# Decode attention and MLP on one core: the MLP's first product moved behind the last contraction, and the output product moved into a section of its own

## The chip, the cores and the metric

The kernel runs on one core of a Trainium2 chip. The core has TensorE (PE in the profile, its weight loads PEld), VectorE (DVE), ScalarE (ACT), GpSimd (POOL), SyncE (SP) and 16 DMA engines, which carry data between HBM and the on-chip memory SBUF. TensorE writes to PSUM. The metric is the device time of one execution in microseconds (us); lower is better. All numbers are float32.

## The reference

One decode step for B = 4 rows of D = 512, with H = 32 heads of 128, and a cache of S = 4096 positions per row and head. Cut to what matters:

```python
xn = layernorm(x)                                  # (4, 1, 512)
# attention on the caches
q = (xn @ wq) as (4, 32, 1, 128)
p = softmax(q . k_cache * 128 ** -0.5)             # over 4096 positions
a = (p . v_cache) as (4, 1, 4096) @ wo             # (4, 1, 512)
# second branch: token mixing, then an MLP of width 1792
x1 = xn + shifted(gelu(layernorm(xn) @ w1)) @ w2   # one position: every shift moves it out, so x1 = xn
m = x1 + gelu(layernorm(x1) @ w3) @ w4
return x + a + m
```

With one position the shifts leave only padding, so w1 and w2 are not needed. The two caches hold 4 x 32 x 4096 x 128 floats each, 268 MB, and each element is used once.

## The kernel before

The 128 pairs of row and head are worked in 32 groups of 4 (`NG`, `HG`). A group's K and its V are 8.4 MB each, laid over 128 partitions. Three buffers of 8.4 MB (`slots` S0, S1, S2) hold everything large: K alternates between S1 and S0, V goes to S2. All large loads are issued by SP, in one queue, in the order in which SP's program has them.

Per group, DVE multiplies K by the query (line 347), sums over the head's 128 elements (line 349) and finds the maximum. ACT makes the softmax weights `pw` and their sums `rs` (line 258). PE contracts `pw` with V in 32 matmuls (`contract`, line 177) into the PSUM tile `pv`. ACT copies `pv` to `os`, and PE's `outputs` (line 183) makes the sums (`ones` x `rs`) and picks the diagonal blocks of `os` with `sel`; ACT copies these to `OS`. PE, ACT and DVE run this in hardware loops (`nc.Fori`).

Behind the loops comes the tail. The last V goes to S1. w3 and w4 go to S2 when its last V is used. wo goes to S0 when the last K is used, in the pieces of `PIECES` (line 72), each with a semaphore of its own. For every row b, DVE normalises `OS` and spreads it into `lt` (lines 359 to 363), PE's `spread` (line 192) turns it by a matmul, and ACT copies it to `X`, the left operand of the product with wo.

The order of the tail is written out by hand, engine by engine, with semaphores between them:

- PE: `spread` of rows 0 to 2, the last group's contraction, its `outputs`, `spread` of row 3, the MLP's first product (x1T x w3 into `pb`, line 211), the second product (gT x w4 into `y`, line 218), the product `ident` x `base` that puts x + xn into `total`, then the product with wo. wo has 32 chunks. Chunks 0 to 23 (`CUT`) are added to `y` in four rows of tiles, chunks 24 to 31 to `total` with four matmuls each. Behind chunk 27, `y`, which ACT has copied to `os` (line 288), is added to `total` by four matmuls with `sel`.
- ACT: the weights, the copies of X for rows 0 to 2, the last group's copies to `os` and `OS`, X for row 3, the copy of `pb` to `hs` (line 283), tanh (line 286), the copy of `y`, two output stores.
- DVE: the normalising of rows 0 to 3, three steps of gelu (lines 366 to 368), three more behind tanh (lines 370 to 372, the last writes gT), and the copy of `total` to `res` (line 374).
- SP: two output stores behind `res`.

All of this is one section (line 119), a block in which every engine has its own program. At its end the engines meet: each drains and signals, POOL releases them, and SP collects a second round of signals. A second section holds one wait of SP, for the output stores (line 377). Then the kernel ends with a further meeting and the clearing of semaphores.

Of the kernel before, what the change touches and what calls it, by code (L numbers as in the profile page):

```python
# [20 lines left out]
def decode_block(ctx: ExitStack, tc: tile.TileContext, x, k, v, wq, wo, w3, w4, out):  # L21
# [47 lines left out]
    def take(e, s, n=1):  # L69
        e.wait_ge(s, n).then_inc(s, -n)  # L70

    PIECES = ((0, 16), (16, 24), (24, 28), (28, 31), (31, 32))
    CUT = 24
    s_x, s_w3, s_w4, s_v, s_vl, s_out = (sem(n) for n in ("sx", "sw3", "sw4", "sv", "svl", "sout"))
    s_wq = [sem(f"swq{n}") for n in range(2)]
# [35 lines left out]
    def part(t):  # L111
        return slice(t * P, (t + 1) * P)

    def store(e, tt):
        e.wait_ge(d_r, 1)
        for t in tt:
            e.dma_start(out_r[:, part(t)], res[32 * t:32 * t + B, :]).then_inc(s_out, 16)

    with tc.tile_critical(no_gpsimd_drain=True), nc.Block(no_gpsimd_drain=True) as block:

        @block.sync
        def _(e):
            def load_k(g):
                e.dma_start(KS[g % 2][:, :], group(kf, g)).then_inc(s_k[g % 2], 16)

            wq_r = wq.rearrange("(p c) n -> p c n", p=P)
            for n in range(2):
                c = slice(n * NC // 2, (n + 1) * NC // 2)
                e.dma_start(wq_sb[:, c, :], wq_r[:, c, :]).then_inc(s_wq[n], 16)
            load_k(0)  # L130
            e.wait_ge(d_Q, 1)
            load_k(1)
            for g in range(NG - 1):
                if g > 0:
                    take(e, v_free)
                e.dma_start(S2[:, :], group(vf, g)).then_inc(s_v, 16)
                if g + 2 < NG:
                    take(e, k_free[g % 2])
                    load_k(g + 2)
            take(e, k_free[0])  # L140
            e.dma_start(S1[:, :], group(vf, NG - 1)).then_inc(s_vl, 16)
            take(e, v_free)
            e.dma_start(w3_sb, w3.rearrange("(p c) f -> p c f", p=P)).then_inc(s_w3, 16)
            e.dma_start(w4_sb, w4.rearrange("(p m) n -> p m n", p=P)).then_inc(s_w4, 16)
            take(e, k_free[1])
            wo_r = wo.rearrange("(p c) n -> p c n", p=P)
            for n, (c0, c1) in enumerate(PIECES):
                e.dma_start(wo_sb[:, c0:c1, :], wo_r[:, c0:c1, :]).then_inc(s_wo[n], 16)
            store(e, (0, 1))

        @block.gpsimd
        def _(e):
# [7 lines left out]

        @block.tensor
        def _(e):
            def mm(o, l, r, start, stop):
                return e.matmul(o, l, r, start=start, stop=stop)  # L164

            e.wait_ge(d_xT, 1)
            for c in range(NC):
                if c % (NC // 2) == 0:
                    e.wait_ge(s_wq[c // (NC // 2)], 16)
                w = wq_sb[:, c, :].rearrange("p (n j h d) -> p n h j d", n=2, j=JB // 2, h=HG)  # L170
                for n in range(2):
                    for h in range(HG):
                        i = mm((pa, pb)[n][32 * h:32 * h + 32, :], xnT[:, c, :], w[:, n, h], c == 0, c == NC - 1)
                    if c == NC - 1:
                        i.then_inc(p_q, 1)

            def contract(V):
                for g in range(G4):
                    t = g % 4
                    i = mm(pv[32 * t:32 * t + 32, :], pw[:, g, :], V[:, 4 * g:4 * g + 4, :], g < 4, g >= G4 - 4)  # L180
                return i

            def outputs(done):
                i = mm(oz[:, HG:2 * HG], ones[:, :], rs[:, :], True, True)
                if done is not None:
                    i.then_inc(done, 1)
                take(e, a_os)
                for m in range(4):
                    i = mm(oz[:, 0:HG], os[:, m, :], sel[:, HG * m:HG * m + HG], m == 0, m == 3)
                i.then_inc(p_oz, 1)  # L190

            def spread(b):
                take(e, d_lt)
                mm(pa[:, 32 * b:32 * b + 32], lt[:, :, :], sel[:, :], True, True).then_inc(p_x, 1)

            with nc.Fori(0, NG - 1, 1, engines=[ET.PE]):
                take(e, s_v, 16)
                take(e, a_w)
                contract(V3).then_inc(p_pv, 1)
                outputs(v_free)  # L200
            for b in range(B - 1):
                spread(b)
            take(e, a_w)
            e.wait_ge(s_vl, 16)
            contract(VL).then_inc(p_pv, 1)
            outputs(None)
            spread(B - 1)
            e.wait_ge(s_w3, 16)
            for c in range(NC):
                for t in range(4):  # L210
                    i = mm(pb[32 * t:32 * t + 32, :FT], x1T[:, c, :], w3_sb[:, c, t * FT:(t + 1) * FT],
                           c == 0, c == NC - 1)
            i.then_inc(p_up, 1)
            e.wait_ge(s_w4, 16)
            e.wait_ge(d_g, 1)
            for m in range(NF):
                t = m % 4
                mm(y[32 * t:32 * t + 32, :], gT[:, 32 * m:32 * m + 32], w4_sb[:, m, :], m < 4, False)
            mm(total[:, 0:P], ident[:, :], base[:, :], True, False)
            e.wait_ge(a_X, 1)  # L220
            for n, (c0, c1) in enumerate(PIECES):
                e.wait_ge(s_wo[n], 16)
                for c in range(c0, c1):
                    if c < CUT:
                        t = (c + 2) % 4
                        i = mm(y[32 * t:32 * t + B, :], X[:, c, :], wo_sb[:, c, :], False, c >= CUT - 4)
                        if c == CUT - 1:
                            i.then_inc(p_y, 1)
                    else:
                        for t in range(4):  # L230
                            i = mm(total[32 * t:32 * t + B, 0:P], X[:, c, :], wo_sb[:, c, part(t)], False, c == WC - 1)
                if c1 == 28:
                    e.wait_ge(a_y, 1)
                    for t in range(4):
                        mm(total[32 * t:32 * t + 32, 0:P], sel[:, :], os[:, t, :], False, False)
            i.then_inc(p_tot, 1)

        @block.scalar
        def _(e):
# [22 lines left out]
            def outputs(o):  # L262
                take(e, p_pv)
                e.copy(os[:, :, :], pv[:, :].rearrange("p (m d) -> p m d", m=4)).then_inc(a_os, 1)  # L264
                take(e, p_oz)
                return e.copy(o, oz[:, 0:2 * HG].unsqueeze(1))  # L266

            def spread(b):
                take(e, p_x)
                return e.copy(X[:, :, b], pa[:, 32 * b:32 * b + 32])  # L270
# [6 lines left out]
            e.drain().then_inc(a_end, 1)  # L277
            for b in range(B - 1):
                spread(b).then_inc(a_lt, 1)
            outputs(OS[:, NG - 1:NG, :]).then_inc(a_end, 1)  # L280
            spread(B - 1).then_inc(a_X, 1)
            e.wait_ge(p_up, 1)
            e.copy(hs.rearrange("p (m i) -> p m i", i=32),
                   pb[:, :FT].rearrange("p (i m) -> p m i", i=32)).then_inc(a_up, 1)
            e.wait_ge(d_u, 1)
            e.activation(gt, gu, AF.Tanh, scale=GELU_A).then_inc(a_t, 1)
            e.wait_ge(p_y, 1)
            e.copy(os[:, :, :], y[:, :].rearrange("p (m d) -> p m d", m=4)).then_inc(a_y, 1)
            store(e, (2, 3))

        @block.vector
        def _(e):
# [60 lines left out]
                    own(e.transpose(mt[:, :], mx[:, :]))  # L353
                    e.tensor_reduce(st[:, 1:2], mt[:, :], axis=AX.X, op=ALU.max, negate=True).then_inc(d_m, 1)  # L354

            for b in range(B):
                e.wait_ge(a_end, 2 if b == B - 1 else 1)
                o = OS[:, b * JB:(b + 1) * JB, :]
                own(e.reciprocal(rec[:, :, :], o[:, :, HG:]))  # L359
                own(e.tensor_mul(ot[:, :, :], o[:, :, 0:HG], rec[:, :, :]))  # L360
                if b > 0:
                    e.wait_ge(a_lt, b)
                e.tensor_mul(lt[:, :, :], ot[:, :, :].rearrange("p j h -> p (j h)").unsqueeze(2).to_broadcast([P, H, 4]),
                             mask[:, :].unsqueeze(1).to_broadcast([P, H, 4])).then_inc(d_lt, 1)
            e.wait_ge(a_up, 1)
            own(e.tensor_mul(gu, hs, hs))
            own(e.tensor_scalar(gu, gu, GELU_B, 1.0, op0=ALU.mult, op1=ALU.add))
            e.tensor_mul(gu, gu, hs).then_inc(d_u, 1)
            e.wait_ge(a_t, 1)
            own(e.tensor_scalar(gt, gt, 1.0, 0.5, op0=ALU.add, op1=ALU.mult))  # L370
            own(e.tensor_mul(hs, hs, gt))
            e.transpose(gT, hs).then_inc(d_g, 1)  # L372
            e.wait_ge(p_tot, 1)
            e.tensor_copy(res[:, :], total[:, 0:P]).then_inc(d_r, 1)  # L374

    with tc.tile_critical(no_gpsimd_drain=True):
        nc.sync.wait_ge(s_out, 64)


# [26 lines left out]
```

## Time and profile before

| | |
|---|---|
| median of 3 runs | 1310.01 us (1309.46 to 1312.22) |
| the profiled execution's own time | 1309.42 us |
| its span, first to last instruction | 1307.6 us |
| DVE busy | 1166.0 us (89%) |
| PE busy | 364.1 us (28%) |
| ACT busy | 98.7 us (8%) |
| read from HBM | 561.02 MB, 429 GB/s over the span |

The page's idle column names what ended an engine's wait; `q` behind an engine's name is its sequencer, which handles waits, branches and DMA issues. In a timeline a row is start (us from the span's start), duration (us), engine, line, operation, tiles, shape and count; a row with a count stands for several instructions merged, and its duration reaches from the first start to the last end. A DMA issue's duration is that of the issue; when the data lands stands in the DMA view. A float32 matmul shows as two instructions. All PE rows have the line of the small helper that issues matmuls, so they are told apart by their tiles. The granted clock of PE is given as a share of full speed.

### The profile page before, as it was taken

The page shows a single profiled execution, that of the slowest core. Times are in us where ns is not written, and L with a number is a line of the kernel's source. Part 1 is how long each engine was busy: PE and PEld are TensorE (multiplying, and loading weights), DVE is VectorE, ACT ScalarE, POOL GpSimd, SP SyncE. Part 2 cuts the span into 40 slices and gives each one's busy share as a digit, 9 for nine tenths or more (in the row PEclk, how much of TensorE's full clock was granted, in tenths as well). Part 3 has the DMA queues.
Part 4 walks back from the last instruction along what each step waited for, and adds up shares of the span by engine and source line. Part 5 has one row for each costly group of instructions (what it writes and reads, how often), then busy time and mean ns, then how long its engine had stood idle before and what let it go on. Part 6 is the DMA issues. An engine that isn't in the chain of part 4 may idle for free. (4 is left out here: it accounts for less than half of the span.)

```text
span 1307.6 us, 6922 instructions
## 1 busy us (share of the span) xinstructions
PE 364.1 (28%) x2622; PEld 130.6 (10%) x2622; DVE 1166.0 (89%) x308; ACT 98.7 (8%) x334; POOL 2.1 (0%) x9
## 2 busy tenths in 40 slices
PE   2032123332113333212333212333311333321256
PEld 0010011110001111001111000111100111100022
DVE  3799999999999999999999999999999999999961
ACT  0000000000000000000000000000000000000010
POOL 0000000000000000000000000000000000000000
PEclk9565566665566666566666556666655666655669
DMA  9999999999999999999999999999999999999997
GB/s 418 417 440 425 443 423 445 421 445 421 445 421 447 421 445 425 441 425 441 429 437 429 437 429 437 429 439 433 433 433 433 437 429 441 425 443 423 443 417 298
DMA packets 10582, 561.11 MB, mean 429 GB/s; under 512 B 1200, under 2 KB 1216, under 8 KB 1488
## 3 DMA queue, kind: packets, MB, share of 16 engines
q1 hardware_dynamic: 10528, 561.00, 99.3%
q8 instruction: 3, 0.05, 0.0%
q10 hardware_dynamic: 48, 0.04, 0.0%
q14 instruction: 3, 0.02, 0.0%
HBM read 561.02 MB, written 0.01 MB: 429 GB/s over the span
## 5 line engine op out<-in xcount | busy, mean ns | idle before, releaser
L347 DVE TENSOR_TENSOR slot<-slot,qb 128x16384 f32<-128x16384 f32 x32 | 551.2, 17226 | 42.4 <-DVEq L70 42.4
L349 DVE TENSOR_REDUCE sc<-slot 128x128 f32<-128x16384 f32 x32 | 551.0, 17220 | 10.5 <-DVEq L70 10.5
L164 PE MATMUL ps<-slot,pw 128*32 128x512 f32 x2048 | 293.5, 737 | 881.1 <-PEq L70 881.1
L164 PEld LDWEIGHTS ps<-slot,pw 128*32 128x32 f32 x2048 | 80.5, 132 | 1068.6 <-issue 1068.5
L258 ACT ACTIVATE pw<-sc,st 32x128 f32<-32x128 f32 x128 | 67.3, 526 | 307.1 <-ACTq L70 305.6
L264 ACT COPY os<-ps 128x512 f32<-128x512 f32 x32 | 18.8, 586 | 798.4 <-ACTq L70 798.4
L164 PE MATMUL ps<-sel,os 128*128 128x4 f32 x256 | 32.8, 252 | 18.1 <-PEq L70 18.1
L164 PEld LDWEIGHTS ps<-sel,os 128*128 128x128 f32 x256 | 31.0, 191 | 19.9 <-issue 19.9
L258 ACT ACTIVATION_READ_ACCUMULATOR pw<-sc,st 32x1 f32 x128 | 26.2, 205 | 0.0
L164 PE MATMUL ps<-slot 128*32 128x512 f32 x92 | 14.8, 788 | 27.8 <-DVE slot L326 22.5
L359 DVE RECIPROCAL rec<-OS 128x32 f32<-128x32 f32 x4 | 1.4, 349 | 14.4 <-ACT OS L266 12.1
L345 DVE STREAM_TRANSPOSE qb<-qx 128x128 f32<-128x128 f32 x32 | 10.0, 312 | 4.7 <-DVEq L70 0.2
L351 DVE TENSOR_REDUCE st<-sc 128x1 f32<-128x128 f32 x32 | 9.2, 286 | 4.7
L164 PE MATMUL ps<-rs,ones 128*128 128x4 f32 x64 | 12.3, 263 | 0.0
L164 PEld LDWEIGHTS ps<-rs,ones 128*128 128x128 f32 x64 | 9.5, 188 | 26.8 <-issue 26.8
L374 DVE COPY res<-ps 128x128 f32<-128x128 f32 x1 | 0.3, 291 | 13.1 <-PE ps L164 13.1
L342 DVE COPY qx<-Q 128x128 f32 x32 | 7.3, 227 | 4.8 <-issue 4.6
L306 DVE TENSOR_REDUCE st<-slot 128x1 f32<-128x512 f32 x2 | 1.4, 686 | 11.3 <-DMA slot<-in_A_x_dram 11.3
L353 DVE STREAM_TRANSPOSE mt<-mx 128x32 f32<-128x32 f32 x32 | 6.8, 211 | 4.7
L354 DVE TENSOR_REDUCE st<-mt 128x1 f32<-128x32 f32 x32 | 5.9, 186 | 4.8 <-DVEq L70 2.1
L352 DVE COPY mx<-st 128x32 f32<-128x32 f32 x32 | 5.8, 182 | 4.7
L266 ACT COPY OS<-ps 128x8 f32 (+1 forms) x32 | 5.3, 166 | 43.7 <-ACTq L70 43.7
(53 smaller groups left out, 49.7 us busy)
## 6 DMA issues: line engine op xcount, KB each, us to landing
slot<-in_A_wq_dram SPq DMA_DIRECT2D x2, 4096.0 KB, 17.2
slot<-in_B_w_dram SPq DMA_DIRECT2D x2, 3584.0 KB, 22.2
slot<-in_A_wo_dram SPq DMA_DIRECT2D x1, 4096.0 KB, 30.5
slot<-in_A_wo_dram SPq DMA_DIRECT2D x1, 2048.0 KB, 35.0
slot<-in_A_wo_dram SPq DMA_DIRECT2D x1, 1024.0 KB, 37.0
slot<-in_A_wo_dram SPq DMA_DIRECT2D x1, 768.0 KB, 38.4
slot<-in_A_k_cache_dram SPq DMA_DIRECT2D x32, 42.3
slot<-in_A_v_cache_dram SPq DMA_DIRECT2D x32, 28.9
```

The source lines that it names most:

```text
L164: return e.matmul(o, l, r, start=start, stop=stop)
L258: i = e.activation(o, sc[r, :].rearrange("p (g w) -> p g w", w=4), AF.Exp, bias=st[r, 1:2], scale=1.0, accum_out=rs[r, h:h + 1])
L264: e.copy(os[:, :, :], pv[:, :].rearrange("p (m d) -> p m d", m=4)).then_inc(a_os, 1)
L266: return e.copy(o, oz[:, 0:2 * HG].unsqueeze(1))
L342: own(e.tensor_copy(qx[:, :].rearrange("p (h r) -> p h r", h=4), Q[:, bass.ds(g + n, 1), :].rearrange("p o h -> p (o h)").unsqueeze(2) .to ...
L345: own(e.transpose(qb[:, :], qx[:, :]))
L347: own(e.tensor_tensor(out=K, in0=K, in1=qb[:, :].unsqueeze(1).to_broadcast([P, C, DH]), op=ALU.mult))
L349: e.reduce_sum(sc[:, :], K, axis=AX.X).then_inc(d_self, 1)
L351: own(e.reduce_max(st[:, 0:1], sc[:, :], axis=AX.X), 2)
L352: own(e.tensor_copy(mx[:, :], st[:, 0:1].to_broadcast([P, 32])))
L353: own(e.transpose(mt[:, :], mx[:, :]))
L354: e.tensor_reduce(st[:, 1:2], mt[:, :], axis=AX.X, op=ALU.max, negate=True).then_inc(d_m, 1)
```

## The change

Four things are done.

- The MLP's first product stands on PE directly behind the last group's contraction; `outputs` and `spread` of row 3 come after it. ACT copies `os`, then `hs`, then `OS`, then does tanh, then X for row 3. DVE does the first three gelu steps ahead of row 3's normalising, and the other three behind it.
- `ident` x `base` comes ahead of the second product.
- wo's first piece of 16 chunks is loaded as two of 8, with a semaphore each. SP issues six pieces in place of five.
- The section with the loops ends behind the second product. The product with wo, the copy of `y`, the copy to `res` and the four stores stand in the second section, which has no block and no loops. PE, ACT and DVE thus pass the meeting at the block's end, and the waits at the second section's entry, ahead of wo. The wait `a_X` in front of wo is gone, since ACT signals the block's end behind the copy of X.

The order of the instructions within wo's product is as before. The diff, cut to its core (`mm` moved out of the tensor program and given the engine as its first argument):

```diff
-    PIECES = ((0, 16), (16, 24), (24, 28), (28, 31), (31, 32))
+    PIECES = ((0, 8), (8, 16), (16, 24), (24, 28), (28, 31), (31, 32))
...
             contract(VL).then_inc(p_pv, 1)
-            outputs(None)
-            spread(B - 1)
             e.wait_ge(s_w3, 16)
             (first product)
             i.then_inc(p_up, 1)
+            outputs(None)
+            spread(B - 1)
+            mm(e, total[:, 0:P], ident[:, :], base[:, :], True, False)
             e.wait_ge(s_w4, 16)
             e.wait_ge(d_g, 1)
             (second product)
-            mm(total[:, 0:P], ident[:, :], base[:, :], True, False)
-            e.wait_ge(a_X, 1)
-            (product with wo)
...
# scalar
-            outputs(OS[:, NG - 1:NG, :]).then_inc(a_end, 1)
-            spread(B - 1).then_inc(a_X, 1)
+            take(e, p_pv)
+            e.copy(os[:, :, :], pv[:, :].rearrange("p (m d) -> p m d", m=4)).then_inc(a_os, 1)
             e.wait_ge(p_up, 1)
             e.copy(hs..., pb...).then_inc(a_up, 1)
+            take(e, p_oz)
+            e.copy(OS[:, NG - 1:NG, :], oz[:, 0:2 * HG].unsqueeze(1)).then_inc(a_end, 1)
             e.wait_ge(d_u, 1)
             e.activation(gt, gu, AF.Tanh, scale=GELU_A).then_inc(a_t, 1)
-            e.wait_ge(p_y, 1)
-            e.copy(os[:, :, :], y[:, :]...).then_inc(a_y, 1)
-            store(e, (2, 3))
+            spread(B - 1).then_inc(a_X, 1)
...
# vector
-            for b in range(B):
+            for b in range(B - 1):
+                normalised(b)
             (three gelu steps)
+            normalised(B - 1)
             e.wait_ge(a_t, 1)
             (three gelu steps)
-            e.wait_ge(p_tot, 1)
-            e.tensor_copy(res[:, :], total[:, 0:P]).then_inc(d_r, 1)
...
     with tc.tile_critical(no_gpsimd_drain=True):
+        e = nc.tensor
+        for n, (c0, c1) in enumerate(PIECES):
+            e.wait_ge(s_wo[n], 16)
+            (the same loop over wo's chunks as before)
+        i.then_inc(p_tot, 1)
+        nc.scalar.wait_ge(p_y, 1)
+        nc.scalar.copy(os[:, :, :], y[:, :]...).then_inc(a_y, 1)
+        nc.vector.wait_ge(p_tot, 1)
+        nc.vector.tensor_copy(res[:, :], total[:, 0:P]).then_inc(d_r, 1)
+        for e, tt in ((nc.sync, (0, 1)), (nc.scalar, (2, 3))):
+            e.wait_ge(d_r, 1)
+            for t in tt:
+                e.dma_start(out_r[:, part(t)], res[32 * t:32 * t + B, :]).then_inc(s_out, 16)
         nc.sync.wait_ge(s_out, 64)
```

More of the change, by code (lines that the diff above doesn't have):

```diff
@@ L112, in part, with mm @@
         return slice(t * P, (t + 1) * P)
[L114 to L117, printed above, removed]
+    def mm(e, o, l, r, start, stop):
+        return e.matmul(o, l, r, start=start, stop=stop)
     with tc.tile_critical(no_gpsimd_drain=True), nc.Block(no_gpsimd_drain=True) as block:
@@ L148, in _ @@
                 e.dma_start(wo_sb[:, c0:c1, :], wo_r[:, c0:c1, :]).then_inc(s_wo[n], 16)
-            store(e, (0, 1))
         @block.gpsimd
@@ L162, in _ @@
         def _(e):
-            def mm(o, l, r, start, stop):
-                return e.matmul(o, l, r, start=start, stop=stop)
             e.wait_ge(d_xT, 1)
@@ L172, in _ @@
                     for h in range(HG):
-                        i = mm((pa, pb)[n][32 * h:32 * h + 32, :], xnT[:, c, :], w[:, n, h], c == 0, c == NC - 1)
+                        i = mm(e, (pa, pb)[n][32 * h:32 * h + 32, :], xnT[:, c, :], w[:, n, h], c == 0, c == NC - 1)
                     if c == NC - 1:
@@ L179, in contract @@
                     t = g % 4
-                    i = mm(pv[32 * t:32 * t + 32, :], pw[:, g, :], V[:, 4 * g:4 * g + 4, :], g < 4, g >= G4 - 4)
+                    i = mm(e, pv[32 * t:32 * t + 32, :], pw[:, g, :], V[:, 4 * g:4 * g + 4, :], g < 4, g >= G4 - 4)
                 return i
             def outputs(done):
-                i = mm(oz[:, HG:2 * HG], ones[:, :], rs[:, :], True, True)
+                i = mm(e, oz[:, HG:2 * HG], ones[:, :], rs[:, :], True, True)
                 if done is not None:
@@ L188, in outputs @@
                 for m in range(4):
-                    i = mm(oz[:, 0:HG], os[:, m, :], sel[:, HG * m:HG * m + HG], m == 0, m == 3)
+                    i = mm(e, oz[:, 0:HG], os[:, m, :], sel[:, HG * m:HG * m + HG], m == 0, m == 3)
                 i.then_inc(p_oz, 1)
@@ L193, in spread @@
                 take(e, d_lt)
-                mm(pa[:, 32 * b:32 * b + 32], lt[:, :, :], sel[:, :], True, True).then_inc(p_x, 1)
+                mm(e, pa[:, 32 * b:32 * b + 32], lt[:, :, :], sel[:, :], True, True).then_inc(p_x, 1)
             with nc.Fori(0, NG - 1, 1, engines=[ET.PE]):
@@ L210, in _ @@
                 for t in range(4):
-                    i = mm(pb[32 * t:32 * t + 32, :FT], x1T[:, c, :], w3_sb[:, c, t * FT:(t + 1) * FT],
+                    i = mm(e, pb[32 * t:32 * t + 32, :FT], x1T[:, c, :], w3_sb[:, c, t * FT:(t + 1) * FT],
                            c == 0, c == NC - 1)
             i.then_inc(p_up, 1)
+            outputs(None)
+            spread(B - 1)
+            mm(e, total[:, 0:P], ident[:, :], base[:, :], True, False)
             e.wait_ge(s_w4, 16)
@@ L217, in _ @@
                 t = m % 4
-                mm(y[32 * t:32 * t + 32, :], gT[:, 32 * m:32 * m + 32], w4_sb[:, m, :], m < 4, False)
-            mm(total[:, 0:P], ident[:, :], base[:, :], True, False)
-            e.wait_ge(a_X, 1)
[L221 to L236, printed above, removed]
+                mm(e, y[32 * t:32 * t + 32, :], gT[:, 32 * m:32 * m + 32], w4_sb[:, m, :], m < 4, False)
         @block.scalar
@@ L284, in _ @@
                    pb[:, :FT].rearrange("p (i m) -> p m i", i=32)).then_inc(a_up, 1)
+            take(e, p_oz)
+            e.copy(OS[:, NG - 1:NG, :], oz[:, 0:2 * HG].unsqueeze(1)).then_inc(a_end, 1)
             e.wait_ge(d_u, 1)
             e.activation(gt, gu, AF.Tanh, scale=GELU_A).then_inc(a_t, 1)
-            e.wait_ge(p_y, 1)
-            e.copy(os[:, :, :], y[:, :].rearrange("p (m d) -> p m d", m=4)).then_inc(a_y, 1)
-            store(e, (2, 3))
+            spread(B - 1).then_inc(a_X, 1)
         @block.vector
@@ L354, in _, with normalised @@
                     e.tensor_reduce(st[:, 1:2], mt[:, :], axis=AX.X, op=ALU.max, negate=True).then_inc(d_m, 1)
-            for b in range(B):
+            def normalised(b):
                 e.wait_ge(a_end, 2 if b == B - 1 else 1)
@@ L372, in _ @@
             e.transpose(gT, hs).then_inc(d_g, 1)
-            e.wait_ge(p_tot, 1)
-            e.tensor_copy(res[:, :], total[:, 0:P]).then_inc(d_r, 1)
     with tc.tile_critical(no_gpsimd_drain=True):
+        e = nc.tensor
+        for n, (c0, c1) in enumerate(PIECES):
+            e.wait_ge(s_wo[n], 16)
+            for c in range(c0, c1):
+                if c < CUT:
+                    t = (c + 2) % 4
+                    i = mm(e, y[32 * t:32 * t + B, :], X[:, c, :], wo_sb[:, c, :], False, c >= CUT - 4)
+                    if c == CUT - 1:
+                        i.then_inc(p_y, 1)
+                else:
+                    for t in range(4):
+                        i = mm(e, total[32 * t:32 * t + B, 0:P], X[:, c, :], wo_sb[:, c, part(t)], False, c == WC - 1)
+            if c1 == 28:
+                e.wait_ge(a_y, 1)
+                for t in range(4):
+                    mm(e, total[32 * t:32 * t + 32, 0:P], sel[:, :], os[:, t, :], False, False)
+        i.then_inc(p_tot, 1)
+        nc.scalar.wait_ge(p_y, 1)
+        nc.scalar.copy(os[:, :, :], y[:, :].rearrange("p (m d) -> p m d", m=4)).then_inc(a_y, 1)
+        nc.vector.wait_ge(p_tot, 1)
[4 more added lines that the diff above has]
+                e.dma_start(out_r[:, part(t)], res[32 * t:32 * t + B, :]).then_inc(s_out, 16)
         nc.sync.wait_ge(s_out, 64)
```

## The prediction

> **What bounds the kernel now.** I read the page first, for the span and the load on the DMA engines, then the DMA view for when each weight block lands, and then the timeline of the last 47 us, where every instruction that the change moves is found.
>
> ```profile
> span 1307.6 us, 6922 instructions
> PE 364.1 (28%) x2622; PEld 130.6 (10%) x2622; DVE 1166.0 (89%) x308; ACT 98.7 (8%) x334; POOL 2.1 (0%) x9
> ...
> DMA  9999999999999999999999999999999999999997
> ...
> HBM read 561.02 MB, written 0.01 MB: 429 GB/s over the span
> ```
>
> All but the last fortieth of the span has the DMA engines at 90% or more. The 561 MB set the time, and no byte of them goes away. What can move is the stretch from the last byte to the end of the span.
>
> ```profile
> slot<-in_A_wo_dram SPq DMA_DIRECT2D x1, 4096.0 KB, 30.5
> slot<-in_A_wo_dram SPq DMA_DIRECT2D x1, 2048.0 KB, 35.0
> ...
> slot<-in_A_wo_dram SPq DMA_DIRECT2D x1, 256.0 KB, 38.5
> ```
>
> ```profile
> L148 SPq DMA_DIRECT2D slot<-in_A_wo_dram x5: 328/426/433, 1260.9 to 1262.7; - x5
> ```
>
> ```profile
> L144 SPq DMA_DIRECT2D slot<-in_B_w_dram x1: 425/425/425, 1255.4 to 1255.4; - x1
> ...
> DMA to landing us min/median/max: 26.3/26.3/26.3
> ```
>
> The five wo pieces are issued from 1260.9 to 1262.7. The first lands at 1260.9 + 30.5 = 1291.4, the last at 1262.7 + 38.5 = 1301.2. w4 lands at 1255.4 + 26.3 = 1281.7.
>
> ```profile
> 1269.23 9.15 PE L164 MATMUL ps<-slot,pw 128*32 128x512 f32 x64
> ...
> 1278.31 0.39 PE L164 MATMUL ps<-rs,ones 128*128 128x4 f32 x2
> 1278.55 0.59 ACT L264 COPY os<-ps 128x512 f32<-128x512 f32 x1 [8.90 <-ACTq L70]
> ...
> 1279.28 1.03 PE L164 MATMUL ps<-sel,os 128*128 128x4 f32 x8 [0.58 <-PEq L70]
> 1280.42 0.17 ACT L266 COPY OS<-ps 128x8 f32<-128x8 f32 x1 [1.29 <-ACTq L70]
> 1280.62 0.35 DVE L359 RECIPROCAL rec<-OS 128x32 f32<-128x32 f32 x1 [12.07 <-ACT OS L266]
> ...
> 1281.46 0.29 DVE L363 TENSOR_TENSOR lt<-ot,mask 128x128 f32<-128x128 f32 x1
> ...
> 1281.90 0.38 PE L164 MATMUL ps<-sel,lt 128*128 128x32 f32 x2 [1.60 <-PEq L70]
> ...
> 1282.21 3.21 PE L164 MATMUL ps<-slot,x1T 128*32 128x448 f32 x32
> ...
> 1285.49 0.53 ACT L283 COPY slot<-ps 128x448 f32<-128x448 f32 x1 [2.87 <-PE ps L164]
> 1286.06 0.62 DVE L366 TENSOR_TENSOR slot<-slot 128x448 f32<-128x448 f32 x1 [4.30 <-ACT slot L283]
> ...
> 1287.37 0.63 DVE L368 TENSOR_TENSOR slot<-slot 128x448 f32<-128x448 f32 x1
> 1288.03 0.58 ACT L286 ACTIVATE slot<-slot 128x448 f32<-128x448 f32 x1 [2.01 <-DVE slot L368]
> ...
> 1289.95 0.65 DVE L372 STREAM_TRANSPOSE slot<-slot 128x448 f32<-128x448 f32 x1
> ...
> 1290.74 5.20 PE L164 MATMUL ps<-slot 128*32 128x512 f32 x28 [5.32 <-DVE slot L372]
> ...
> 1295.87 0.49 PE L164 MATMUL ps<-base,ident 128*128 128x128 f32 x2
> ...
> 1296.29 6.21 PE L164 MATMUL ps<-slot,X 128*4 128x512 f32 x80
> ...
> 1302.57 1.06 PE L164 MATMUL ps<-slot,X 128*4 128x128 f32 x32
> 1303.70 0.29 DVE L374 COPY res<-ps 128x128 f32<-128x128 f32 x1 [13.10 <-PE ps L164]
> 1304.01 0.67 SPq L117 DMA_DIRECT2D out_dram<-res  x2
> ```
>
> The reader is to see that wo's product starts at 1296.29, 4.9 us after its first piece is there, and then runs without a gap to 1302.57 + 1.06 = 1303.63, 2.4 us after the last piece. In this tail PE is late and the DMA is not. PE is late because the chain 1282.21 (MLP's first product), gelu, 1290.74 (second product) stands behind the last group's `outputs` and `spread`. Nothing more than about 2.1 us can be won ahead of the end, because behind the last landing the last four matmuls are due in any case.
>
> **Step 1: MLP's first product right behind the contraction.** The contraction ends at 1269.23 + 9.15 = 1278.38. The first product takes its 3.21, and w3 and x1T are there (it waited for neither at 1282.21). It ends at 1281.6 (was 1285.42). ACT copies `os` at 1278.55 beside it, then `hs` at 1281.7 to 1282.2. PE goes on with the sums and `sel` products, 0.39 + 1.03, to 1283.0; ACT's copy of OS, which now stands behind `hs`, ends at 1283.3. DVE does the three gelu steps from 1282.25; they took 1286.06 to 1288.00, so 1.94, and end at 1284.2. Tanh follows on ACT to 1284.8. DVE meanwhile does the last row's normalising, 1280.62 to 1281.75 = 1.13, to 1285.35. That is 0.55 behind tanh, and this 0.55 is what the new order of DVE costs the gelu chain. The three steps behind tanh took 1288.61 to 1290.60 = 1.99, so gT is ready at 1287.35, 3.25 earlier. `spread` (0.38) on PE and the copy of X on ACT, now behind tanh, end near 1286.2, and the product with `ident` (0.49) ends there too: both lie in PE's wait for gT. If that cover were gone they would cost 0.9.
>
> **Step 2: the second product.** It starts at 1287.45 and w4 has long landed. How long it takes hangs on the clock:
>
> ```profile
> 1283.71:1287.12 3.41, 1.71 (x20) 0.39 (x12) 0.92 (x2) 0.53 (x1) 0.00 (x0) 1.00 1.06 452
> 1287.12:1290.53 3.41, 0.00 (x0) 0.00 (x0) 2.33 (x5) 0.58 (x1) 0.00 (x0) 1.00 0.89 380
> 1290.53:1293.95 3.42, 3.21 (x16) 0.90 (x20) 0.07 (x1) 0.00 (x0) 0.00 (x0) 0.50 0.96 405
> 1293.95:1297.36 3.41, 3.41 (x30) 1.01 (x26) 0.00 (x0) 0.00 (x0) 0.00 (x0) 1.00 0.99 408
> ```
>
> The columns are the stretch, its length, busy PE, PEld, DVE, ACT and POOL, the granted clock, the DMA share and GB/s. After a stretch of 3.41 us without PE work the clock is 0.50, and after a busy one 1.00 again. At 0.50, 16 of the 28 instructions fill the 3.21, so all would take 5.6. At 1.00, where the first product ran to its end, 32 of 448 columns took 3.21, so 28 of 512 would take 3.2. In the new order PE has small matmuls alone from 1281.6 to 1287.45, 5.9 us, so I expect a drop again and take the 5.20 of the row. It ends at 1292.65, with 1290.65 and 1293.05 as bounds.
>
> [...]
>
> **Step 3: the border of the sections.** New between the second product and wo are the drain and semaphore round of the block's end and the entry waits of the second section. Before, the same round stands behind the output writes:
>
> ```profile
> L119 ACTq EVENT_SEMAPHORE  x2: 17/17/17, 1305.3 to 1305.5; - x2
> ...
> L119 SPq NOP  x1: 18/18/18, 1305.8 to 1305.8; - x1
> ```
>
> ```profile
> L401 SPq COMPARE_BRANCH  x1: 38/38/38, 1306.2 to 1306.2; - x1
> ```
>
> From the last arrival (ACT, 1305.3) to SP's branch it takes 0.9; PE's own semaphore steps and branch are slower:
>
> ```profile
> L196 PEldq COMPARE_BRANCH  x31: 76/208/233, 92.2 to 1255.6; - x31
> ```
>
> I add this branch (0.2) and 0.2 for its waits, so 1.3. SP, POOL, ACT and DVE arrive before PE: SP's last issue is over at 1263.1, or 0.43 later with the sixth piece, and DVE ends at 1287.35. The lower bound is 0.9. Above, a fetch of code may be added:
>
> ```profile
> q8 instruction: 1, 0.02, 2.0%
> ```
>
> That is the instruction queue between 1299 and 1302: 2.0% of 16 engines x 3 us = 0.96 for one packet. So 0.9 to 2.3. I take 1.3, since the loop's branch shows 0.2 and no fetch. wo then starts at 1293.95 (bounds 1291.55 and 1295.35).
>
> **Step 4: wo and its first piece in two.** At 429 GB/s the first 2 MB land some 4.9 us before 1291.4, the second half at 1291.4. PE is there at 1293.95, later than both, so the split is worth nothing; the extra issue (0.43 on SP) is hidden by a queue that is some 20 us deep (w4, issued before, lands at 1281.7). From start to end wo took 1303.63 - 1296.29 = 7.34. From 1293.95 PE would be done at 1301.3. The last piece lands at 1301.2 and its 8 of the 32 instructions of 1.06 take 0.27, with the 0.14 that PE took to start behind gT (1290.60 to 1290.74): 1301.6. So the landing is late next, and PE ends 2.05 earlier.
>
> **Step 5: the end.** Copy and issue of the output stay as they are. The round of step 3 no longer stands between the issue's end (1304.68) and the wait for the writes, which was over by the branch at 1306.2. So the writes hide between none and all of 1.5; the second section's own end costs SP a few waits that it did not have, so -0.2 is possible too. I take 0.2, near the lower end, since a write has to reach HBM and come back in any case.
>
> **The sum.** 2.05 + 0.2 = 2.25. The profiled execution took 1309.42 us (its span and 1.8 around it), 0.6 below the median of the runs shown, 1310.01. That gives 1307.2 for it and 1307.7 for the median.
>
> **The rivals.**
> First, PE stays the bound: the second product runs at half clock to its end (5.6) and the border costs 2.3. wo starts at 1295.35 and ends at 1302.7; with step 5 the gain is 1.1 and the time 1308.9. With half of these surcharges it is 1302.0 and 1308.2. For it speaks that step 4 has only 0.3 to spare.
> Second, the end gives more: the output writes were done early and nearly all of step 5's 1.5 is won. Then the gain is 3.3: 1306.6. Against it: the writes are new traffic on an idle queue, and nothing shows how long they take.
> Third, the other side: the border leaves PE idle long enough for the clock to fall, and wo begins at 0.50. The 1.3 idle alone are well below the 3.41 of the empty stretch; with one fetch it is 2.3, with two 3.2, and from about there it decides. The price is 0.96 or 1.9 for the fetches and 3.41 us at half rate, so 1.7, up to twice that: wo ends at 1304.0 to 1306.6, later than 1303.63, and the time is 1310.2 to 1312.7. Against it stands the branch of 0.2.
> [...]
>
> **How the numbers follow.** Forecast 0.52, PE the bound 0.22, a shorter end 0.16, slower 0.10. About 0.2% (2.6 us) is what a measurement of this kernel can tell from no change; the runs shown spread over 2.8. The forecast's 2.25 lies 0.4 below that, so I give 0.24 of its 0.52 to faster and 0.28 to the same; the shorter end is faster, PE as the bound is the same, and the slower case splits 0.02 and 0.08. So 0.40, 0.52 and 0.08. The range reaches from 0.6 below the second rival, 1306.0, to the beginning of the third, 1310.6; the forecast's own is 1306.9 to 1308.5.
>
> **What would show it.** The first product (line 115, x1T) should start within 0.1 of the contraction's end, gT's transpose (line 353) should end some 9.0 behind it, and the second product begin there. From that product's end to wo's first matmul should be 1.3; 2.3 or more means a fetch. wo's last matmuls should wait for the sixth piece and end 0.4 behind its landing, at 1301.6 if the DMA stands as before. A clock of 0.50 in wo would be the third rival. Wrong would be the forecast if the landing itself moves, since steps 1 to 3 then only shift the wait.

## The result, and the profile after

The changed kernel takes 1307.01 us (median of 7 runs, 1305.89 to 1307.20) against 1311.58 us of the kernel before in the same comparison (7 runs, 1309.46 to 1313.15). The ratio is 0.9964, with a 95% interval of 0.9953 to 0.9976: faster by 0.36%. The profiled execution took 1307.07 us, with a span of 1305.3 us. Against the profiled execution of before (1309.42 us) that is 2.35 us less; between the medians it is 4.6 us. Where the other 2.2 us come from is the question of the experiments. The ratio isn't taken from the two medians, which would give 0.9965.

The page of the changed kernel, its chain that ended last:

```profile
DMA 3%; SPq 0%; PE 0%; issue 0%; DVE 0%
DMA slot<-in_A_wo_dram 3%; SPq L146 0%; PE ps L115 0%; DVE res L376 0%
```

The chain no longer runs through gelu and PE's products. It runs back from the last copy through a few matmuls to a landing of wo. In order of time (start, duration, what):

```profile
1261.30 39.18 DMA slot<-in_A_wo_dram
1300.48 0.04 issue
1300.52 1.10 PE ps L115 x32
```

The timeline of the tail (start, duration, engine, line, operation, tiles, shape, count, idle time before and what ended it):

```profile
1267.80 8.77 PE L115 MATMUL ps<-slot,pw 128*32 128x512 f32 x64
...
1276.39 3.18 PE L115 MATMUL ps<-slot,x1T 128*32 128x448 f32 x32
...
1282.07 0.35 DVE L336 RECIPROCAL rec<-OS 128x32 f32<-128x32 f32 x1
1282.19 0.58 ACT L265 ACTIVATE slot<-slot 128x448 f32<-128x448 f32 x1 [1.12 <-DVE slot L348]
...
1283.11 0.38 DVE L351 TENSOR_SCALAR slot<-slot 128x448 f32<-128x448 f32 x1
...
1284.42 0.65 DVE L353 STREAM_TRANSPOSE slot<-slot 128x448 f32<-128x448 f32 x1
1285.21 5.16 PE L115 MATMUL ps<-slot 128*32 128x512 f32 x28 [1.19 <-DVE slot L353]
1291.50 3.62 PE L115 MATMUL ps<-slot,X 128*4 128x512 f32 x32 [1.13 <-SPq L355]
1296.19 1.90 PE L115 MATMUL ps<-slot,X 128*4 128x512 f32 x16 [1.08 <-DMA slot<-in_A_wo_dram]
...
1298.68 1.06 PE L115 MATMUL ps<-slot,X 128*4 128x128 f32 x32 [0.59 <-DMA slot<-in_A_wo_dram]
...
1300.52 1.06 PE L115 MATMUL ps<-slot,X 128*4 128x128 f32 x32 [0.57 <-DMA slot<-in_A_wo_dram]
1301.64 0.29 DVE L376 COPY res<-ps 128x128 f32<-128x128 f32 x1 [16.58 <-PE ps L115]
```

PE now waits three times for a piece of wo, 1.08 + 0.59 + 0.57 = 2.2 us in all, where before it ran without a gap. These are the third, fourth and fifth of the six pieces. The issues of wo by their line, and the last piece in the DMA view (size, us to landing):

```profile
L146 SPq DMA_DIRECT2D slot<-in_A_wo_dram x6: 327/428/433, 1259.5 to 1261.8; - x6
```

```profile
slot<-in_A_wo_dram SPq DMA_DIRECT2D x1, 256.0 KB, 39.3
```

The last piece lands at 1261.8 + 39.3 = 1301.1, within 0.1 of where it landed before, and PE is done at 1300.52 + 1.06 = 1301.58. The landing that holds PE is not this one but that of the piece before it, at 1300.48: from there PE runs its last 32 instructions in the 1.06 that they also took before, without a wait among them. The last 8 of these need the last piece, and it is there when their turn comes.

### The profile page after: what moved, and what is told of

Its sections match the earlier page's. It is cut to its first block, busy times and chain, and to the rows that moved or that the text cites. A ratio compares the mean times of both kernels' runs of the same rounds, so it can differ in the third digit from the quotient of the medians.

```text
span 1305.3 us, 6940 instructions
## 1 busy us (share of the span) xinstructions
PE 367.8 (28%) x2622; PEld 131.0 (10%) x2622; DVE 1165.8 (89%) x308; ACT 98.6 (8%) x334; POOL 2.1 (0%) x9
## 5 line engine op out<-in xcount | busy, mean ns | idle before, releaser
L115 PE MATMUL ps<-slot,pw 128*32 128x512 f32 x2048 | 298.1, 747 | 875.3 <-PEq L70 875.3
L115 PE MATMUL ps<-slot,X 128*4 128x128 f32 (+1 forms) x112 | 7.6, 410 | 3.4 <-DMA slot<-in_A_wo_dram 2.2
## 6 DMA issues: line engine op xcount, KB each, us to landing
slot<-in_A_wo_dram SPq DMA_DIRECT2D x1, 256.0 KB, 39.3
```

## The experiments

The theory at this point: before, PE ends the tail late; the new order on PE, ACT and DVE lets the landing end it; the section's border and the split add little; and what the median gained beyond the profiled pair is the granted clock, which costs the kernel before more in most executions than in the profiled one. The rivals: the border moved out of the end is the gain; or the landing itself differs between executions.

### The new order alone

One section and five pieces; PE, ACT and DVE in the order of the change.

```diff
             contract(VL).then_inc(p_pv, 1)
-            outputs(None)
-            spread(B - 1)
             (first product).then_inc(p_up, 1)
+            outputs(None)
+            spread(B - 1)
+            mm(total[:, 0:P], ident[:, :], base[:, :], True, False)
             (second product; a_X; product with wo, as before)
```

> The new order on PE, ACT and DVE alone: one section, five pieces of wo. Theory (the tail of before waits for PE, and the new order makes it wait for the last landing instead): gT 3.2 us earlier behind the contraction, the product with wo starts some 1.1 us earlier than in the changed kernel, waits for its last pieces, and ends 0.4 to 0.5 us behind the last landing; the time is that of the changed kernel plus 0 to 0.4 us, about 1307.3 us. Rival (the gain comes from the section's border moved out of the end): at most 1 us faster than before.

It took 1307.14 us (7 runs, 1307.07 to 1307.59) against 1309.99 us of before, a ratio of 0.9974 (0.9962 to 0.9985). Its timeline:

```profile
1296.48 1.90 PE L164 MATMUL ps<-slot,X 128*4 128x512 f32 x16 [0.74 <-DMA slot<-in_A_wo_dram]
...
1300.79 1.06 PE L164 MATMUL ps<-slot,X 128*4 128x128 f32 x32 [0.56 <-DMA slot<-in_A_wo_dram]
1301.91 0.29 DVE L381 COPY res<-ps 128x128 f32<-128x128 f32 x1 [15.02 <-PE ps L164]
```

PE waits for pieces of wo here too, and ends 0.47 behind the last landing, as in the changed kernel. The order alone brings the time within 0.13 us of the changed kernel's first median and 0.40 of its second (below). That compares runs from different comparisons, not all on one chip, and the unchanged kernel's own medians lie between 1309.90 and 1311.64 in them. By ratios, each to before in its own comparison, it is 0.9974 against 0.9964 and 0.9968, with intervals that overlap. So the order has most of the gain, and a small share of the border or the split isn't excluded by this run.

### The border alone

The order and the pieces of before; the product with wo, the last copies and the stores in the second section.

```diff
             mm(e, total[:, 0:P], ident[:, :], base[:, :], True, False)
-            e.wait_ge(a_X, 1)
-            (product with wo, the copies of y and total, the stores)
     with tc.tile_critical(no_gpsimd_drain=True):
+        (product with wo, the copies of y and total, the stores)
         nc.sync.wait_ge(s_out, 64)
```

> The order of before, five pieces, but the product with wo and the stores in the second section. Theory: PE is the bound, so the 1.1 us of the border, measured between the second product and wo in the changed kernel, lie on the path; the shorter end gives back 0.2 to 0.3 us. About 0.9 us slower than before. Rival (the border is what gains): 1 us or more faster than before.

The median is 1311.75 us (12 runs, 1308.86 to 1313.64), the ratio 1.0004 (0.9994 to 1.0014). That agrees with the 0.9 us expected (1.0007), but an unchanged copy of before gave 1.0008 (0.9999 to 1.0017) in the same comparison, so a cost of this size can't be told from none. A gain of 1 us (0.9992) lies outside the interval, so the rival of the border falls. What the run showed beside it is its profiled execution, which took 1313.64 us:

```profile
1282.10 5.91 PE L115 MATMUL ps<-slot,x1T 128*32 128x448 f32 x32
1293.35 5.83 PE L115 MATMUL ps<-slot 128*32 128x512 f32 x28 [5.33 <-DVE slot L346]
1300.82 6.21 PE L115 MATMUL ps<-slot,X 128*4 128x512 f32 x80 [1.22 <-SPq L348]
```

The border is there, 1.22 ahead of wo. But the MLP's first product, which no part of this edit touches, took 5.91 in place of 3.21.

### The kernel before, profiled again

> The kernel before once more, unchanged, for a second profile of it. Theory: where the time is above 1309.5 us, the last landing is still near 1301.2 us and the surplus lies in PE's tail behind the contraction: the second product or the product with wo has more of its instructions at a clock of 0.50, or the contraction starts later. Rival: the last landing itself is later, by the whole surplus.

Twelve runs of the unchanged kernel gave 1309.03 to 1313.11 us, with a median of 1311.64. The profiled one took 1311.72. Its tail, its issues of wo and its last piece:

```profile
1267.81 9.57 PE L164 MATMUL ps<-slot,pw 128*32 128x512 f32 x64
...
1281.43 5.72 PE L164 MATMUL ps<-slot,x1T 128*32 128x448 f32 x32
...
1292.48 5.74 PE L164 MATMUL ps<-slot 128*32 128x512 f32 x28 [5.33 <-DVE slot L372]
...
1304.85 1.06 PE L164 MATMUL ps<-slot,X 128*4 128x128 f32 x32
```

```profile
L148 SPq DMA_DIRECT2D slot<-in_A_wo_dram x5: 328/425/434, 1259.5 to 1261.3; - x5
```

```profile
slot<-in_A_wo_dram SPq DMA_DIRECT2D x1, 256.0 KB, 38.7
```

The last landing is at 1261.3 + 38.7 = 1300.0, 1.2 earlier than in the first profile, and PE ends at 1305.9, 2.3 later. So the surplus is not the landing. It is PE: 5.9 us behind the landing, not 2.4. The windows of this tail tell why (stretch, length, PE, PEld, DVE, ACT, POOL busy, granted clock, DMA share, GB/s):

```profile
1272.88:1276.29 3.41, 3.41 (x36) 0.97 (x32) 0.00 (x0) 0.00 (x0) 0.00 (x0) 1.00 0.96 412
1276.29:1279.70 3.41, 2.42 (x22) 1.39 (x14) 0.09 (x1) 0.75 (x2) 0.00 (x0) 1.00 1.06 454
1279.70:1283.12 3.42, 2.23 (x14) 1.10 (x18) 0.75 (x3) 0.22 (x1) 0.00 (x0) 0.50 0.98 422
1283.12:1286.53 3.41, 3.41 (x24) 0.79 (x17) 0.00 (x0) 0.00 (x0) 0.00 (x0) 0.50 1.08 456
```

Between the contraction's end at 1277.38 and the first product at 1281.43 PE has only the narrow matmuls of `outputs` and `spread`. The clock fell to 0.50 at 1279.70, ahead of the first product, and came back at 1286.53, 0.6 ahead of its end: 5.72 in place of 3.21, so 2.5 us on the path. Of the other 1.0 us, 0.42 lie in the contraction (9.57 for 9.15) and 0.54 in the second product (5.74 for 5.20); a longer part of each ran at 0.50 (5.07 us of the contraction for 4.24, and at least 4.29 of the second product for 3.21). In the first profile the clock fell only at the end of the gelu wait, at 1290.53. A third profile took 1313.32 us.

> The kernel before, unchanged, for a third profile. Theory: the first product takes 3.2 us where the granted clock stays 1.00 up to it and more where it has fallen ahead of it, and the end follows: behind the last landing by 2.4 us in the first case, and by up to 6 us in the second.

Its first product took 5.83 and began at 1282.94, 1.5 behind the fall of the clock, and PE ended 6.4 us behind the last landing, a little more than expected.

```profile
1282.94 5.83 PE L164 MATMUL ps<-slot,x1T 128*32 128x448 f32 x32
```

```profile
1278.02:1281.43 3.41, 2.21 (x22) 1.26 (x10) 0.30 (x1) 0.75 (x2) 0.00 (x0) 1.00 0.99 424
1281.43:1284.85 3.42, 2.45 (x14) 1.10 (x18) 0.53 (x3) 0.22 (x1) 0.00 (x0) 0.50 1.02 441
```

The 21 runs that stand for the kernel before in this comparison reach from 1307.7 to 1314.3.

### Keeping PE busy in its waits

Before, with five extra matmuls in the gelu wait. Their results aren't read; they are work that the kernel doesn't need.

```diff
             i.then_inc(p_up, 1)
+            for n in range(5):
+                mm(pv[:, :], pw[:, 0:4, :], w3_sb[:, 0, 0:512], True, True)
             e.wait_ge(s_w4, 16)
```

> Before, with five extra matmuls of 128 x 512 on PE between the MLP's first and second product, where PE waits some 5 us for the gelu; their result is never read. Theory (part of what PE loses in before is the granted clock, which falls to 0.50 in this wait, at a point that differs from run to run): the clock stays 1.00, the second product takes some 3.2 us in place of 5.2 or more, wo starts 2 us earlier and ends near the last landing; 2 to 4 us faster than the median of before, and a narrow spread as in the changed kernel. Rival (the clock is no part of it): no change, or slower by what the extra matmuls hold up.

1307.56 us, ratio 0.9981 (0.9970 to 0.9991). In its profile the second product took 3.63:

```profile
1289.49 3.63 PE L165 MATMUL ps<-slot 128*32 128x512 f32 x28 [0.83 <-DVE slot L375]
1293.46 6.21 PE L165 MATMUL ps<-slot,X 128*4 128x512 f32 x80
```

Its weight loads start in groups 0.42 to 0.43 us apart from 1289.92 to 1292.06, as those of the contraction did at 1.00 in the second profile of before (0.43; 0.86 at 0.50), so 3.63 is this product's time at full clock, and the 3.2 of the prediction's lower bound was too low. The product with wo follows at once. The spread was not narrow: five runs lie at 1306.55 to 1307.60, three at 1308.88 to 1309.98. By the theory these three lost their clock in the other wait, ahead of the first product, but none of them was profiled. Two more extra matmuls there:

```diff
             outputs(None)
-            spread(B - 1)
             e.wait_ge(s_w3, 16)
+            for n in range(2):
+                mm(y[:, :], pw[:, 0:4, :], w3_sb[:, 0, 0:512], True, True)
+            spread(B - 1)
```

> Before, with the five extra matmuls between the MLP's two products, and two more between the last group's outputs and spread, where PE waits some 1.5 us for DVE; their results are never read (the two write y, which the second product starts anew). Order, pieces and sections are those of before. Theory (the surplus of before over the last landing is the clock that falls in one of these two waits): the first product takes 3.2 us in every run and no longer 5.7 in some, so the runs lie as close together as those of the changed kernel, without the runs near 1309.9 that the five alone left, and the median is near 1307.3 us although nothing was moved; the two may cost 0.3 us. Rival (the moved order itself is what the gain needs): still some runs near 1310 us, or no gain over the five alone.

1307.30 us (11 runs, 1306.27 to 1308.39), ratio 0.9982 (0.9973 to 0.9991). The runs near 1309.9 are gone. The spread of 2.1 us is wider than expected; its profile has 3.21 for the first product and 3.63 for the second, and PE ends 0.60 behind the last landing, against 0.47 in the changed kernel. With nothing moved and seven useless matmuls added, the median comes within 0.3 to 0.6 us of the changed kernel's. But the runs come from another chip than the changed kernel's second set: against before in its own comparison this kernel wins 2.6 us between medians, the changed one 4.6 and 4.3. So it is shown that holding the clock up wins the kernel before some 2.5 us; whether matmuls without use win as much as the new order is not settled.

### The split, and how much border is free

The changed kernel with wo's first piece whole:

```diff
-    PIECES = ((0, 8), (8, 16), (16, 24), (24, 28), (28, 31), (31, 32))
+    PIECES = ((0, 16), (16, 24), (24, 28), (28, 31), (31, 32))
```

> The changed kernel with wo's first piece whole (five pieces). Theory (the end waits for the last landing, and PE has waits of some 2.2 us ahead of it in the product with wo): the split is worth nothing; the time is that of the changed kernel within 0.3 us, about 1307.0 us. Rival (the split lets wo start earlier, and that counts): 0.5 us or more slower than the changed kernel.

1306.52 us (7 runs), against 1306.74 us of the changed kernel beside it: the split wins nothing that can be seen. The same comparison had the changed kernel once more:

> The changed kernel once more beside the kernel before, on the same chip as the three others. Theory: its runs lie within some 1.5 us of each other, since the last landing bounds them and PE's clock no longer does; those of before are spread over 3 us or more. Rival: both are spread alike.

Its nine runs lie at 1305.79 to 1307.69, those of before at 1308.12 to 1313.18; the ratio is 0.9968 (0.9959 to 0.9978). The spread is 1.9 us against 5.1 (23 runs of before). Then more borders between the second product and wo, one and four:

```diff
+    for _ in range(4):            # once in the other
+        with tc.tile_critical(no_gpsimd_drain=True):
+            nc.tensor.wait_ge(d_g, 1)
+            nc.scalar.wait_ge(a_X, 1)
+            nc.vector.wait_ge(d_g, 1)
+            nc.sync.wait_ge(s_w4, 16)
     with tc.tile_critical(no_gpsimd_drain=True):
         e = nc.tensor
```

> The changed kernel with one more section between the second product and the product with wo, which holds only waits that are long fulfilled: one more border, some 0.6 to 1.1 us. Theory: it is taken out of PE's waits for the last pieces, and the time is that of the changed kernel within 0.3 us. Rival (the border lies on the path): slower than the changed kernel by all of its 0.6 to 1.1 us.

1306.94 us, 0.2 from the changed kernel. In its timeline the border is 0.85 longer than in the changed kernel's first profile, and the wait for the next piece shorter by 0.62:

```profile
1291.87 3.62 PE L115 MATMUL ps<-slot,X 128*4 128x512 f32 x32 [1.98 <-SPq L360]
1295.95 1.90 PE L115 MATMUL ps<-slot,X 128*4 128x512 f32 x16 [0.46 <-DMA slot<-in_A_wo_dram]
```

> The changed kernel with four more such sections. PE then stands still for some 3.5 to 5.5 us ahead of wo. Theory: more than the waits of 2.2 us can hide, so wo ends 1 to 3 us behind the changed kernel's end, and if the granted clock falls to 0.50 in this wait, wo's first chunks run at half rate and it is up to 3 us more: 1308 to 1313 us. Rival (PE's lead is larger than the traces show, or the border costs far less): the time of the changed kernel.

1310.50 us (11 runs), 3.8 behind the changed kernel; the profiled one took 1310.08. Timeline and windows:

```profile
1295.56 7.90 PE L115 MATMUL ps<-slot,X 128*4 128x512 f32 x80 [4.16 <-SPq L361]
1303.54 1.06 PE L115 MATMUL ps<-slot,X 128*4 128x128 f32 x32
```

```profile
1291.40:1295.56 4.16, 0.00 (x1) 0.00 (x1) 0.00 (x0) 0.00 (x0) 0.00 (x0) 1.00 0.95 398
1296.07:1299.48 3.41, 3.41 (x24) 0.70 (x20) 0.00 (x0) 0.00 (x0) 0.00 (x0) 0.50 0.67 269
```

PE stands still for 4.16, the clock falls inside wo, to 0.50 from 1296.07 to 1299.48, and wo takes 1304.60 - 1295.56 = 9.04, where it took 7.34 before: 1.7 more. The border's surplus over the changed kernel is 4.16 - 1.13 = 3.0. Of these 4.7 us the waits for the pieces hide some 2, and 3.0 are left between the two profiled executions (1310.08 and 1307.07); between the medians it is 3.8, and the other 0.8 was not traced.

## Why the prediction was right or wrong

The time was near: 1307.0 for 1307.7, and the tail came nearly as worked out. Between the profiled executions 2.25 us were forecast and 2.35 came. The size of the gain between the medians was wrong by half: the measured one is 0.36%, 4.6 us, and the case that was given the largest chance, no change beyond 0.2%, is not the one that came.

- **Step 1** held. The first product starts with the contraction's end (1276.57), and gT is ready at 1285.07, 8.5 behind it; 9.0 was said. The difference is a first product that overlaps the contraction's end by 0.2, and row 3's normalising, which holds the gelu chain up by 0.34 (tanh ends at 1282.77, the next step starts at 1283.11) and not by 0.55.
- **Step 2** held in this execution: the clock fell once (0.50 from 1284.92 to 1288.33) and the second product took 5.16, for 5.20. Both bounds were too low: for 3.2 at full clock the runs with extra matmuls show 3.63, and for 5.6 the other two profiles of before show 5.74 and 5.79. Neither counted here.
- **Step 3**: 1.13 for 1.3 in the profile, 1.22 in the run with the border alone. No run shows the fetch of code that the bound of 2.3 (0.96 for one) and the third rival add here: in the changed kernel's profile the instruction queue moved nothing from 1290 to 1292, where the border lies.
- **Step 4** held: the split is worth nothing, a landing ends the tail, and PE is done at 1301.58, for 1301.6. The landing is another than the one that was said: PE waits for the fifth piece at 1300.48 and has 1.06 of matmuls behind it, while the sixth, at 1301.11, holds nothing up. That the two sums give the same end is luck. The waits are larger than the 0.3 to spare that I gave: wo's product starts at 1291.50 and not at 1293.95, since in this execution the contraction began 1.4 earlier (1267.80, not 1269.23) and took 8.77, not 9.15, and since gT came 0.5 sooner behind it. That the last landing stood where it did before (1301.1 for 1301.2), though the tail began earlier, is luck as well.
- **Step 5**: from PE's end to the span's end it took 1307.6 - 1303.63 = 4.0 before and 1305.3 - 1301.58 = 3.7 after. 0.2 was said.
- **The sum** is what failed, in its last sentence: the gain against one profiled execution, 2.25, was taken off the median of the runs, so the changed kernel's median was put 0.5 above its profiled execution, after the 0.6 of before. It came out 0.06 below it (1307.01 and 1307.07). The profiled execution of before was one in which the clock stayed up through the first product. Others of before lose 2.5 us there alone. The new order removes this loss too, since the first product now stands right behind 8.77 us of wide matmuls and takes 3.18, and what the second product still loses lies in waits. The unchanged kernel lost its clock at the end of the gelu wait in one profile (1290.53) and ahead of the first product in two others (1279.70 and 1281.43). Step 2 asked what the clock does to the changed kernel's second product alone. The same should have been asked of the kernel before.
- **The rivals.** PE as the bound did not come, with 2.2 us of waits in PE. The shorter end did not come, with 0.3 us in step 5. What the third rival feared came in the run with five borders: PE stood still for 4.16, the clock was 0.50 in wo, and the price was the 1.7 that the rival gave. One border, 1.13 in the changed kernel, did not bring it: there the clock was 1.00 from 1288.33 to PE's end.

That the clock accounts for the runs of before that nobody profiled is inferred from three profiles of before, the one with the border alone, and the two runs with extra matmuls; it wasn't seen in each run. Part of their spread is DMA: the last landing lay at 1301.2 and 1300.0 in the first two profiles of before and within these 1.4 us, from 1300.0 to 1301.4, in all twelve profiles. What moves it was not tried. In the five profiles of the new order without extra sections or with one, PE ends 0.46 to 0.47 behind it each time.

## What to carry to other kernels

One profiled execution is one sample of what differs between executions: before taking a saving off a median, ask where in its own spread the profiled run lies, and behind which of its waits the granted clock may have fallen (here at 1279.70, 1281.43 and 1290.53 in three profiles of one kernel). Work for PE that was ready early did better here right behind 8.77 us of wide matmuls than behind a chain of small ones: the first product took 3.18 in the changed kernel, and 3.21, 5.72 and 5.83 in the three profiles of before. With the order left as it was, matmuls without use in the waits won back part of the loss (2.4 and 2.6 us between medians). A border between sections cost PE 1.13 and 1.22 here, and where PE then waited for a DMA anyway, one more made no difference that can be seen (1306.94 for 1306.74).

## What was not expected of the hardware

The granted clock fell to 0.50 at the end of a stretch in which PE was busy for 2.42 of 3.41 us by the trace (1276.29 to 1279.70 in the second profile of before), while in the first it stayed at 1.00 past a stretch with 1.71 busy (1283.71 to 1287.12). The 1.71 was all wide matmuls, of 448 columns. In the other stretch the wide ones ended at 1277.38, so 1.09, and the rest were matmuls of 4 columns, which the trace shows as some 250 ns each. So in these two the time of wide matmuls fits what the clock did and the busy time does not. In the first profile the clock also stayed at 1.00 past 1300.78 to 1304.19, where matmuls of 128 columns are most of the 2.85 busy. That is a reading of three stretches: no run varied the width by itself.
